# One decode layer on one core: the tail after the last attention head rearranged (order of the last loads, form of the w2 products, output rows, spare products)

## The chip, the cores and the metric

The kernel runs on one core of one Trainium2 chip. The metric is device time in microseconds (us), the median of several executions. A profile's span is some 1.8 us shorter than the device time of the same execution, so spans are compared with spans and times with times. In the views PE is TensorE, which does the matrix products, and PEld its loading of weights; DVE, ACT and POOL are the vector, scalar and GpSimd engines, and SP issues the loads. The granted clock is the share of its full clock (1.00) that TensorE was allowed.

## The reference, cut to what matters

One token is decoded: a modulated layernorm, attention with 8 key/value heads over a cache of 32768 positions, and a feed-forward part with relu.

```python
mod = (silu(c) @ w_mod)                       # six vectors of 512: sa, ca, ga, sb, cb, gb
h = layernorm(x) * (1 + ca) + sa
x = x + ga * (attention(h @ wq, k_cache, v_cache) @ wo)   # wq 512x4096, wo 4096x512
h = layernorm(x) * (1 + cb) + sb
x = x + gb * (relu(h @ w1) @ w2)              # w1 512x1792, w2 1792x512
```

The caches are 134 MB of bf16; with the weights 149.4 MB are read. Everything from "@ wo" on is small work that needs the last head's result. It is called the tail here.

## The kernel before

All loads go through one queue on SP in a fixed order, into a ring of four slots of 4 MB. A load waits until the earlier user of its slot is done.

```python
WOP = [(0, Hkv // 2), (Hkv // 2, Hkv // 4), (3 * Hkv // 4, Hkv // 4)]   # wo in three parts, by heads
W2P = [(0, FA - 3), (FA - 3, 2), (FA - 1, 1)]                          # w2 in three pieces
ring = ctx.enter_context(tc.tile_pool(name="ring", bufs=4))
...
stream += [("v", LAST, (0, 1)), ("v", LAST, (2,)), ("wo", 0), ("v", LAST, (3,)), ("wo", 1), ("wo", 2)]
stream += [("w1",)] + [("w2", i) for i in range(len(W2P))]
```

P·V of a head is done with 512-column products, whose result (`o_ps`) has to be gathered by `blocks` (four operations on DVE) and `o_cols` (a product) into columns. Only the last quarter of the last head is done with 64 small products that write the columns at once. The w2 products go to four column groups: the four of a block write partitions 0, 32, 64 and 96 and run side by side. `normalise` and `spread` then prepare the columns for the products with wo. Part 0 of wo gives rows, which `join_rows` turns into columns; this is done around the wait for the last V.

```python
pv(LAST, (2,))
blocks(LAST)
project(0)            # wo, part 0: 16 row products
o_cols(LAST)
join = join_rows()
next(join)            # copy of the rows on ACT
pv(LAST, (3,))        # 64 small products, straight into the columns
next(join); next(join)
normalise(LAST)
for _ in join: pass
for i in range(1, len(WOP)): project(i)
# ... x1T, layernorm, w1 products into hidT, then w2 on four column groups:
nc.tensor.matmul(ffn_ps[32 * i:32 * i + 1, :], lhsT=hidT[:, ft:ft + 1], rhs=w2_sb[:, a, b, i * P:(i + 1) * P], ...)
# ... two DVE operations, then the output from partitions 0, 32, 64, 96:
nc.scalar.dma_start(out=out[0, 0].rearrange("(i n) -> i n", i=KT), in_=o_bf[:].rearrange("(i r) n -> i r n", r=32)[:, 0, :])
```

## Time and profile before

| | before |
|---|---|
| time, median (3 runs) | 355.85 us (355.77 to 356.11) |
| span of the profiled execution | 354.3 us |
| transfers | 149.4 MB, 432 to 433 GB/s in the middle |
| clock of TensorE over the span | 0.919 |
| x1T starts / w1's products / w2's last product ends | 343.40 / 346.05 to 347.70 / 350.86 us |

The last product group is 24 products, 16 of the next to last piece and 8 of the last; the 8 start at 350.48 only, and the page's list of DMA issues has 7.1 us from issue to landing for that piece, which was issued at 343.40. So the last landing was near 350.4. The transfers themselves still moved a little until about 350.2.

### The profile page before, as it was taken

How to read it: one execution, taken by the hardware profiler on the slowest of the kernel's cores; microseconds unless marked ns; L12 is line 12 of the kernel's file. 1: busy time of each engine (PE TensorE's matmuls, PEld its weight loads, DVE VectorE, ACT ScalarE, POOL GpSimd, SP SyncE). 2: the span in 40 equal slices, each digit the busy share in tenths (PEclk: the TensorE clock that was granted, in tenths of full speed). 3: DMA queues.
4: the chain of work that ended last, by engine and by line, in shares of the span. 5: the costliest groups of instructions: out<-in, count | busy, mean ns of one | idle time of the engine just before them, and what ended most of it. 6: DMA issues, size and time to landing. Idle time of an engine off the chain costs nothing. (4 is left out here: it accounts for less than half of the span.)

```text
span 354.3 us, 4169 instructions
## 1 busy us (share of the span) xinstructions
PE 276.4 (78%) x1403; PEld 114.0 (32%) x1403; DVE 205.8 (58%) x266; ACT 28.9 (8%) x70; POOL 8.4 (2%) x14
## 2 busy tenths in 40 slices
PE   0453793799798979897979796989789787989884
PEld 0121231233233323332333233333333233333373
DVE  8537683973848366571949177553938095843221
ACT  1023004000110011001100101010100010010110
POOL 9000000000000000000000000000000000000000
PEclk9966867699899999999999998899999999999955
DMA  8999999999999999999999999999999999999994
GB/s 313 449 422 455 420 426 451 422 429 425 446 429 414 459 425 416 459 422 422 455 422 425 442 433 426 436 436 422 425 451 425 422 453 425 422 455 403 424 418 164
DMA packets 6613, 149.61 MB, mean 422 GB/s; under 512 B 712, under 2 KB 712, under 8 KB 1608
## 3 DMA queue, kind: packets, MB, share of 16 engines
q1 hardware_dynamic: 6592, 149.43, 98.2%
q8 instruction: 9, 0.15, 0.1%
q14 instruction: 4, 0.03, 0.0%
q10 hardware_dynamic: 8, 0.00, 0.0%
HBM read 149.42 MB, written 0.00 MB: 422 GB/s over the span
## 5 line engine op out<-in xcount | busy, mean ns | idle before, releaser
L398 DVE STREAM_TRANSPOSE KTt<-Ksb 128x2048 f32<-128x2048 f32 x64 | 143.3, 2283 | 61.9 <-DMA Ksb<-in_A_k_cache_dram 52.6
L489 PE MATMUL o_ps<-Vsb,PT_g 128*16 (+1 forms) x496 | 124.9, 387 | 23.4 <-ACT qbd L382 7.8
L418 PE MATMUL S_ps<-KTt,qbd 128*128 128x512 bf16 x512 | 124.1, 395 | 17.9 <-DVE KTt L398 16.2
L418 PEld LDWEIGHTS <-qbd 128*128 128x128 bf16 x512 | 50.0, 100 | 83.3 <-issue 27.4
L489 PEld LDWEIGHTS o_ps<-Vsb,PT_g 128*16 x416 | 36.4, 87 | 90.9 <-issue 66.4
L424 DVE TENSOR_SCALAR_CACHE_REDUCE S_g<-S_ps 128x512 f32<-128x512 f32 x16 | 11.1, 691 | 29.2 <-PE S_ps L418 29.2
L382 ACT COPY qbd<-qrep_sb 32x128 bf16<-32x128 bf16 x32 | 9.4, 295 | 137.1 <-PE S_ps L418 136.0
L461 DVE STREAM_TRANSPOSE PT_g<-P_g 128x1024 bf16<-128x1024 bf16 x8 | 9.7, 1218 | 6.5 <-ACT P_g L455 6.5
L452 ACT ACTIVATE nbias<-Mb_ps 128x1 f32<-128x1 f32 x8 | 1.4, 171 | 130.8 <-PE Mb_ps L450 130.8
L489 PEld LDWEIGHTS <-PT_g 128*16 128x16 bf16 x80 | 6.9, 90 | 10.1 <-issue 0.8
L219 PE MATMUL xc_ps<-cx_sel,cx_bd 16*128 16x2 bf16 x4 | 0.3, 172 | 12.1 <-DVE cx_bd L213 12.1
L455 ACT ACTIVATE P_g<-S_g,nbias 128x1024 bf16<-128x1024 f32 x8 | 9.2, 1149 | 0.2
L520 DVE SCALAR_TENSOR_TENSOR Y<-o_ps,smask,Y 16x128 f32<-16x128 f32 x24 | 8.0, 335 | 0.8
L159 DVE COPY sel<-ident_bf 128x128 bf16<-128x128 bf16 x4 | 7.5, 3688 | 0.0
L541 DVE TENSOR_TENSOR oT_sb<-acc_ps,Linv 128x4 bf16<-128x4 f32 x8 | 1.2, 151 | 9.4 <-PE acc_ps L528 5.6
L467 PE MATMUL L_ps<-Lexp,ones_f 128*128 128x4 f32 x16 | 3.0, 258 | 4.3 <-DVE Lexp L464 4.3
L439 DVE TENSOR_REDUCE Mrow<-mT_ps 1x4 f32<-1x128 f32 x8 | 2.1, 257 | 6.9 <-PE mT_ps L436 6.9
L355 PE MATMUL q_ps<-wq_sb,hT 128*1 128x512 bf16 x32 | 3.6, 625 | 3.0 <-DVE hT L270 3.0
L436 PE MATMUL mT_ps<-ident_f,m_p 128*1 128x128 f32 x8 | 2.2, 270 | 3.9 <-DVE m_p L433 2.0
L467 PEld LDWEIGHTS L_ps<-Lexp,ones_f 128*128 128x128 f32 x16 | 3.1, 222 | 5.7 <-issue 5.1
L287 PE MATMUL mod_ps<-wm_sb,siluT 128*1 128x512 bf16 x24 | 3.4, 612 | 1.2 <-DVE siluT L281 1.2
L510 DVE MEMSET o_ps<- 16x512 f32 x8 | 3.9, 485 | 0.8
(115 smaller groups left out, 84.4 us busy)
## 6 DMA issues: line engine op xcount, KB each, us to landing
Ksb<-in_A_k_cache_dram SPq DMA_DIRECT2D x16, 4096.0 KB, 29.8
Vsb<-in_A_v_cache_dram SPq DMA_DIRECT2D x15, 4096.0 KB, 24.2
wq_sb<-in_A_wq_dram SPq DMA_DIRECT2D x1, 4096.0 KB, 18.7
Vsb<-in_A_v_cache_dram SPq DMA_DIRECT2D x2, 2048.0 KB, 17.9
wm_sb<-in_w_mod_dram SPq DMA_DIRECT2D x1, 3072.0 KB, 10.3
wo_sb<-in_A_wo_dram SPq DMA_DIRECT2D x1, 2048.0 KB
wo_sb<-in_A_wo_dram SPq DMA_DIRECT2D x2, 1024.0 KB, 8.0
w_sb<-in_B_w_dram SPq DMA_DIRECT2D x1, 1792.0 KB, 10.7
```

What stands on the lines that cost most here:

```text
L159: nc.vector.tensor_copy(out=sel[:, hp, :].rearrange("p (a c) -> p a c", a=4), in_=src)
L355: nc.tensor.matmul(q_ps[i][32 * a:32 * a + 1, :].rearrange("o (h e) -> o h e", e=32), lhsT=hT[:, kt:kt + 1], rhs=wq_f[:, kt, i, a], start= ...
L382: nc.scalar.copy(out=o, in_=i)
L398: t = nc.vector.transpose(out=KTt[:].bitcast(F32), in_=Ksb[:, 32 * half:32 * half + 32, :].rearrange("p j d -> p (j d)").bitcast(F32),)
L418: nc.tensor.matmul(S_ps_tiles[g], lhsT=qbd[g % 2][:, hp, s, :], rhs=KTv[:, 16 * sl:16 * sl + 16, h, :, par], start=(t4 == 0 and sl == 0 an ...
L424: nc.vector.tensor_scalar(out=S_tiles[g][:, G, :], in0=S_ps_tiles[g], scalar1=1.0, scalar2=None, op0=ALU.mult, op1=ALU.max, accum_out=m_ti ...
L455: nc.scalar.activation(out=P_g[:], in_=S_g[:].rearrange("p g f -> p (g f)"), func=ACT.Exp, bias=nbias[:], scale=scale, accum_out=l_g[:],)
L461: nc.vector.transpose(out=PT_g[:], in_=P_g[:])
L467: nc.tensor.matmul(L_ps[:], lhsT=ones_f[:], rhs=Lexp[:], start=True, stop=True)
L489: nc.tensor.matmul(o_tiles[g][:], lhsT=PT, rhs=Vx, start=False, stop=False, skip_group_check=True)
L510: nc.vector.memset(o_tiles[g][:], 0.0)
L520: nc.vector.scalar_tensor_tensor(out=Y[:], in0=o[:, s], scalar=smask[:, s:s + 1], in1=Y[:], op0=ALU.mult, op1=ALU.add,)
```

## The change

Its intent: V of the last head complete earlier, only a small part of wo left after it; the last landing of w2 followed by few products; the output read from neighbouring partitions; and products without use ("spare", 22 of them) that keep TensorE at full clock through the waits of the tail. Besides, the whole tail is put in program order, w1 is loaded in two parts and its products are ordered by quarters of the input (kt), and the copy of x1's rows moves from ACT to DVE. The diff, cut to its core:

```diff
-    WOP = [(0, Hkv // 2), (Hkv // 2, Hkv // 4), (3 * Hkv // 4, Hkv // 4)]
+    WOP = [(0, Hkv // 2), (Hkv // 2, Hkv // 4), (Hkv - 2, 1), (Hkv - 1, 1)]
+    WOROWS = 2
-    W2P = [(0, FA - 3), (FA - 3, 2), (FA - 1, 1)]
+    W2P = [(0, 2, slice(0, FB)), (2, FA - 5, slice(0, FB)), (FA - 3, 1, slice(0, FB)), (FA - 2, 1, slice(0, FB)),
+           (FA - 1, 1, slice(0, 1)), (FA - 1, 1, slice(1, FB))]
+    W1P = [(0, KT - 1), (KT - 1, KT)]
@@ the queue (w2's last four pieces get buffers of their own)
-    stream += [("v", LAST, (0, 1)), ("v", LAST, (2,)), ("wo", 0), ("v", LAST, (3,)), ("wo", 1), ("wo", 2)]
+    stream += [("v", LAST, (0, 1)), ("v", LAST, (2, 3))] + [("wo", i) for i in range(len(WOP))]
@@ spare products
+    def keep_clock(n):
+        for _ in range(n):
+            nc.tensor.matmul(spare[0], lhsT=ident_bf[:], rhs=qbd[0][:, 0, 0:4, :], start=True, stop=True)
@@ the tail
-        pv(LAST, (2,))
+        pv(LAST, (2, 3))
         blocks(LAST)
         project(0)
+        keep_clock(2)
         o_cols(LAST)
-        join = join_rows() ... pv(LAST, (3,)) ...
+        keep_clock(4)
         normalise(LAST)
+        project(1)          # now rows, like part 0
+        keep_clock(3)
+        join_rows()         # all of it here
+        keep_clock(1)
+        project(2)
+        keep_clock(2)
+        project(3)
+        ... keep_clock(4); layernorm_T(...); keep_clock(3); w1 by kt with 2 spares; relu; keep_clock(1)
@@ w2: block-diagonal columns of h, one column group, four neighbouring rows
-                        ffn_ps[32 * i:32 * i + 1, :], lhsT=hidT[:, ft:ft + 1],
+                            ffn_ps, lhsT=hid_bd[:, ft, i, :], rhs=w2_sb[:, a, b - bs.start, i * P:(i + 1) * P],
-        in_=o_bf[:].rearrange("(i r) n -> i r n", r=32)[:, 0, :],
+    nc.scalar.dma_start(out=out[0, 0].rearrange("(i n) -> i n", i=KT), in_=o_bf[:])
```

More of the change, by code (lines that the diff above doesn't have):

```diff
@@ L104, in load @@
         elif kind == "w1":
-            t = ring.tile([P, KT, Dff], BF16, tag="slot", name="w1_sb")
-            src = w1_v
-        else:
-            a0, n = W2P[key[1]]
-            t = ring.tile([P, n, FB, D], BF16, tag="slot", name="w2_sb")
-            src = w2_v[:, a0:a0 + n]
+            k0, k1 = W1P[key[1]]
+            t = ring.tile([P, k1 - k0, Dff], BF16, tag="slot", name="w1_sb")
+            src = w1_v[:, k0:k1]
+        else:
+            a0, n, bs = W2P[key[1]]
+            if key[1] < 2:
+                t = ring.tile([P, n, FB, D], BF16, tag="slot", name="w2_sb")
+            else:
+                t = const.tile([P, n, bs.stop - bs.start, D], BF16, name=f"w2_sb{key[1]}")
+            src = w2_v[:, a0:a0 + n, bs]
         stream_dma(t[:], src)
@@ L129 @@
             stream += [(kind, gg, (2 * G, 2 * G + 1)) for kind, gg in (("k", g + 1), ("v", g))]
-    stream += [("v", LAST, (0, 1)), ("v", LAST, (2,)), ("wo", 0), ("v", LAST, (3,)), ("wo", 1), ("wo", 2)]
-    stream += [("w1",)] + [("w2", i) for i in range(len(W2P))]
+    stream += [("v", LAST, (0, 1)), ("v", LAST, (2, 3))] + [("wo", i) for i in range(len(WOP))]
+    stream += [("w1", i) for i in range(len(W1P))] + [("w2", i) for i in range(len(W2P))]
     pos = [0]
@@ L197 @@
     )
-    rowpick = const.tile([P, P], F32)
-    nc.gpsimd.memset(rowpick[:], 0.0)
+    rowpick = const.tile([P, KT], F32)
     nc.vector.tensor_reduce(
-        out=rowpick[:].rearrange("p (j m) -> p j m", m=32)[:, :, 0],
-        in_=ident_f[:].rearrange("p (j m) -> p j m", m=32), op=ALU.add, axis=AX.X,
-    )
+        out=rowpick[:], in_=ident_f[:].rearrange("p (j m) -> p j m", m=32), op=ALU.add, axis=AX.X,
+    )
+    hid_bd = const.tile([P, FT, KT, KT], BF16)
+    nc.gpsimd.memset(hid_bd[:], 0.0)
     rowsum = const.tile([P, 1], F32)
@@ L249, in layernorm_T @@
         stat_ps = small_ps([P, 2], f"stat_ps_{tagp}")
-        m = nc.tensor.matmul(stat_ps[:], lhsT=onesD_f[:], rhs=stat_in[:], start=True, stop=True)
-        tc.stamp_issue_order_token(m.ins, "pe_tail")
+        nc.tensor.matmul(stat_ps[:], lhsT=onesD_f[:], rhs=stat_in[:], start=True, stop=True)
         nu = const.tile([P, KT], F32, name=f"nu_{tagp}")
@@ L261, in layernorm_T @@
         std = const.tile([P, 1], F32, name=f"std_{tagp}")
-        a = nc.scalar.activation(out=std[:], in_=negvar[:], func=ACT.Sqrt, bias=eps_t[:], scale=-1.0)
-        tc.stamp_issue_order_token(a.ins, "act_tail")
+        nc.scalar.activation(out=std[:], in_=negvar[:], func=ACT.Sqrt, bias=eps_t[:], scale=-1.0)
         cen = const.tile([P, KT], F32, name=f"cen_{tagp}")
@@ L313, with four_rows @@
         )
-    def rows32(src_T, name):
+    def four_rows(src_T, name, copy):
         e = const.tile([P, 32, KT], F32, name=f"{name}_exp")
@@ L322, in rows32 @@
         )
-        r_ps = bank(f"{name}_ps")[:, 0:P]
-        m = nc.tensor.matmul(
+        r_ps = bank(f"{name}_ps")[0:KT, 0:P]
+        nc.tensor.matmul(
             r_ps, lhsT=rowpick[:], rhs=e[:].rearrange("p m kt -> p (m kt)"), start=True, stop=True,
         )
-        tc.stamp_issue_order_token(m.ins, "pe_tail")
-        rows = const.tile([P, P], F32, name=f"{name}_rows")
-        a = nc.scalar.copy(out=rows[:], in_=r_ps)
-        tc.stamp_issue_order_token(a.ins, "act_tail")
+        rows = const.tile([KT, P], F32, name=f"{name}_rows")
+        copy(out=rows[:], in_=r_ps)
         return rows
-    gb_rows = rows32(modT_sb[:, 5 * KT:6 * KT], "gb")
+    gb_rows = four_rows(modT_sb[:, 5 * KT:6 * KT], "gb", nc.scalar.copy)
     hT = const.tile([P, KT], BF16)
@@ L477, in pv @@
         Vs = [need(("v", g, u)) for u in us]
-        if g == LAST and us[0] == NTILE - 1:
-            for j in range(TK):
-                c0 = REP * (4 + j // 16)
-                nc.tensor.matmul(
-                    oT_ps, lhsT=Vs[0][:, j, :], rhs=PT_g[:, j % 16, c0:c0 + REP],
-                    start=False, stop=(j == TK - 1), skip_group_check=True,
-                )
-            return
         def step(u, V, PT, Vx):
@@ L523, in blocks @@
         Y_tiles[g] = Y
-        if g == LAST:
-            nc.vector.memset(oT_ps, 0.0)
     def o_cols(g):
         nc.tensor.matmul(
-            oT_ps, lhsT=Y_tiles.pop(g)[:], rhs=qsel, start=(g < LAST), stop=(g < LAST), skip_group_check=True,
+            oT_ps, lhsT=Y_tiles.pop(g)[:], rhs=qsel, start=True, stop=True, skip_group_check=True,
         )
@@ L568, in project @@
         for r in range(n):
-            if i == 0:
+            if i < WOROWS:
                 nc.tensor.matmul(
                     a_rows[0][32 * (r % 4):32 * (r % 4) + 1, :], lhsT=o2_tiles[i][:, r:r + 1],
-                    rhs=wo_sb[:, r, :], start=False, stop=(r >= n - 4), skip_group_check=True,
+                    rhs=wo_sb[:, r, :], start=False, stop=(i == WOROWS - 1 and r >= n - 4), skip_group_check=True,
                 )
@@ L588, in join_rows @@
         for ko in range(KT):
-            yield
             nc.tensor.matmul(
@@ L593, in join_rows @@
             )
+    spare = []
+    def keep_clock(n):
+        if not spare:
+            spare.append(bank("spare_ps"))
+        for _ in range(n):
+            nc.tensor.matmul(spare[0], lhsT=ident_bf[:], rhs=qbd[0][:, 0, 0:4, :], start=True, stop=True)
     with tc.manual_schedule(engines={mybir.EngineType.PE, mybir.EngineType.DVE}):
@@ L661 @@
         normalise(LAST - 1)
-        pv(LAST, (2,))
+        pv(LAST, (2, 3))
         blocks(LAST)
         project(0)
+        keep_clock(2)
         o_cols(LAST)
-        join = join_rows()
-        next(join)
-        pv(LAST, (3,))
-        next(join)
-        next(join)
-        normalise(LAST)
-        for _ in join:
-            pass
-        for i in range(1, len(WOP)):
-            project(i)
-    ffn_ps = bank("ffn_ps")[:, 0:P]
-    nc.vector.memset(ffn_ps, 0.0)
-    stat2 = const.tile([P, 2], F32)
@@ L681 @@
-    x1T = const.tile([P, KT], F32)
-    nc.vector.tensor_tensor(out=x1T[:], in0=attnT_ps, in1=modT_sb[:, 2 * KT:3 * KT], op=ALU.mult)
-    nc.vector.scalar_tensor_tensor(
-        out=x1T[:], in0=x1T[:], scalar=1.0, in1=xT, op0=ALU.mult, op1=ALU.add, accum_out=stat2[:, 0:1],
-    )
-    h2T = const.tile([P, KT], BF16)
-    layernorm_T(x1T[:], stat2, h2T[:], modT_sb[:, 3 * KT:4 * KT], ncb[:], "ln2")
-    x1_rows = rows32(x1T[:], "x1")
-    w1_sb = need(("w1",))
-    w1_f = w1_sb.rearrange("p kt (a m b) -> p kt a b m", m=P, b=FB)
@@ L693 @@
-    hidT_ps = small_ps([P, FT], "hidT_ps")
-    for ft in range(FT):
-        for kt in range(KT):
-            nc.tensor.matmul(
-                hidT_ps[:, ft:ft + 1], lhsT=w1_f[:, kt, ft // FB, ft % FB, :], rhs=h2T[:, kt:kt + 1],
-                start=(kt == 0), stop=(kt == KT - 1),
-            )
-    hidT = const.tile([P, FT], BF16)
-    nc.scalar.activation(out=hidT[:], in_=hidT_ps[:], func=ACT.Relu)
-    for part, (base, n) in enumerate(W2P):
-        w2_sb = need(("w2", part))
-        for a in range(n):
-            for b in range(FB):
-                ft = (base + a) * FB + b
-                for i in range(KT):
+        keep_clock(4)
@@ new lines @@
+        normalise(LAST)
+        project(1)
[5 more added lines that the diff above has]
+        project(3)
+        hidT_ps = small_ps([P, FT], "hidT_ps")
+        nc.vector.memset(hidT_ps[:], 0.0)
+        stat2 = const.tile([P, 2], F32)
+        x1T = const.tile([P, KT], F32)
+        nc.vector.tensor_tensor(out=x1T[:], in0=attnT_ps, in1=modT_sb[:, 2 * KT:3 * KT], op=ALU.mult)
+        nc.vector.scalar_tensor_tensor(
+            out=x1T[:], in0=x1T[:], scalar=1.0, in1=xT, op0=ALU.mult, op1=ALU.add, accum_out=stat2[:, 0:1],
+        )
@@ L708 @@
+        h2T = const.tile([P, KT], BF16)
+        keep_clock(4)
+        layernorm_T(x1T[:], stat2, h2T[:], modT_sb[:, 3 * KT:4 * KT], ncb[:], "ln2")
+        keep_clock(3)
+        for part, (k0, k1) in enumerate(W1P):
+            w1_f = need(("w1", part)).rearrange("p kt (a m b) -> p kt a b m", m=P, b=FB)
+            for kt in range(k0, k1):
+                for ft in range(FT):
                     nc.tensor.matmul(
-                        ffn_ps[32 * i:32 * i + 1, :], lhsT=hidT[:, ft:ft + 1],
@@ L710 @@
-                        rhs=w2_sb[:, a, b, i * P:(i + 1) * P], start=False, stop=(ft == FT - 1),
-                        skip_group_check=True,
-                    )
-    o_rows = const.tile([P, P], F32)
-    nc.vector.tensor_tensor(out=o_rows[:], in0=ffn_ps, in1=gb_rows[:], op=ALU.mult)
-    o_bf = const.tile([P, P], BF16)
-    nc.vector.tensor_tensor(out=o_bf[:], in0=o_rows[:], in1=x1_rows[:], op=ALU.add)
-    nc.scalar.dma_start(
-        out=out[0, 0].rearrange("(i n) -> i n", i=KT),
-        in_=o_bf[:].rearrange("(i r) n -> i r n", r=32)[:, 0, :],
-    )
+                        hidT_ps[:, ft:ft + 1], lhsT=w1_f[:, kt - k0, ft // FB, ft % FB, :], rhs=h2T[:, kt:kt + 1],
@@ new lines @@
+                        start=False, stop=(kt == KT - 1), skip_group_check=True,
+                    )
+                if kt < KT - 2:
+                    keep_clock(1)
+        hb = hid_bd[:]
+        nc.scalar.activation(
+            out=AP(hb.tensor, hb.offset, [hb.ap[0], [KT * KT, FT], [KT + 1, KT]]),
+            in_=hidT_ps[:].unsqueeze(2).to_broadcast([P, FT, KT]), func=ACT.Relu,
+        )
+        x1_rows = four_rows(x1T[:], "x1", nc.vector.tensor_copy)
+        keep_clock(1)
+        ffn_ps = bank("ffn_ps")[0:KT, 0:P]
@@ new lines @@
+        last = len(W2P) - 1
+        for part, (base, n, bs) in enumerate(W2P):
+            w2_sb = need(("w2", part))
+            for a in range(n):
+                for b in range(bs.start, bs.stop):
+                    ft = (base + a) * FB + b
+                    for i in range(KT):
+                        nc.tensor.matmul(
+                            ffn_ps, lhsT=hid_bd[:, ft, i, :], rhs=w2_sb[:, a, b - bs.start, i * P:(i + 1) * P],
+                            start=(part == 0 and a == 0 and b == 0 and i == 0), stop=(ft == FT - 1 and i == KT - 1),
+                        )
@@ L724 @@
+        o_rows = const.tile([KT, P], F32)
+        nc.vector.tensor_tensor(out=o_rows[:], in0=ffn_ps, in1=gb_rows[:], op=ALU.mult)
+        o_bf = const.tile([KT, P], BF16)
+        nc.vector.tensor_tensor(out=o_bf[:], in0=o_rows[:], in1=x1_rows[:], op=ALU.add)
+    nc.scalar.dma_start(out=out[0, 0].rearrange("(i n) -> i n", i=KT), in_=o_bf[:])
 _INS = ['A_x', 'A_k_cache', 'A_v_cache', 'A_wq', 'A_wo', 'B_x', 'B_w1', 'B_w2', 'c', 'w_mod']
```

## The prediction

> **What bounds the kernel now.** I read the page's 40 slices first, then the busy time by stretches, then the chain of waits, and last the timeline of the tail.
>
> ```profile
> PEclk9966867699899999999999998899999999999955
> DMA  8999999999999999999999999999999999999994
> 260.00:300.00 40.00, 33.66 (x144) 12.89 (x143) 23.11 (x26) 1.41 (x3) 0.00 (x0) 1.00 1.00 432
> 336.83:349.85 13.02, 9.86 (x229) 9.20 (x230) 2.24 (x15) 0.96 (x4) 0.00 (x0) 0.53 0.95 389
> ```
>
> The first two lines are the page's slices; the stretches list PE, PEld, DVE, ACT, POOL, the granted clock, the DMA share and GB/s. The transfers are the bound: 149.4 MB pass at 432 to 433 GB/s in every 40 us stretch from 20 to 300 us, and the change moves the same bytes. Only the ends can change. In the last 13 us the rate is 389 GB/s, so 13.02 x (1 - 389/432) = 1.3 us of transfer time is lost there, and TensorE runs at a granted clock of 0.53. After 349.85 us nothing is loaded.
>
> ```profile
> 316.55 5.71 PE o_ps L489 x26
> 322.25 0.03 PE L_ps L467
> 322.29 14.55 DMA Vsb<-in_A_v_cache_dram
> 336.83 0.05 issue
> 336.88 1.81 PE acc_ps L482 x64
> 338.69 0.95 PE acc_ps L590 x4
> ...
> 341.24 1.07 PE acc_ps L576 x32
> 342.31 0.02 issue
> 342.32 7.49 DMA w_sb<-in_B_w_dram
> 349.81 0.04 issue
> 349.85 0.59 PE ffn_ps L708 x16
> ...
> 351.31 0.29 DVE o_bf L716
> ```
>
> The chain (start, length, what) shows that the end is set by the landing of the last piece of w2 at 349.81, which was in the queue behind everything else. From there to the end of the span at 354.3 is 4.5 us: 1.06 products, 0.7 on DVE, and 2.7 from o_bf to the end with the output's DMA. The attention part ends at 343.36, and its second layernorm feeds w1's products just as w1 lands (346.0). So compute and transfers are balanced in the tail: whoever becomes later sets the end.
>
> ```profile
> 323.42 3.83 PE L489 MATMUL o_ps<-Vsb,PT_g 128*16 128x512 bf16 x17 [0.85 <-DVE o_ps L510]
> 335.97 0.38 PE L528 MATMUL acc_ps<-mask_sb,Y 16*128 16x4 f32 x2 [0.76 <-DVE acc_ps L525]
> 343.40 0.16 DVE L682 TENSOR_TENSOR x1T<-acc_ps,modT_sb 128x4 f32<-128x4 f32 x1 [2.86 <-PE acc_ps L576]
> 345.62 0.22 DVE L270 SCALAR_TENSOR_TENSOR h2T<-cen_ln,rstd_ln,modT_sb 128x4 bf16<-128x4 f32 x1
> 346.05 1.65 PE L696 MATMUL hidT_ps<-h2T,w_sb 128*128 128x1 bf16 x56 [0.81 <-DMA w_sb<-in_B_w_dram]
> 348.60 1.02 PE L708 MATMUL ffn_ps<-w_sb,hidT 128*1 128x128 bf16 x32 [0.89 <-DMA w_sb<-in_B_w_dram]
> ```
>
> These timeline lines give my unit costs. A P·V product of 512 columns takes 3.83/17 = 0.22 us at full clock; w1's take 1.65/56 = 0.029 us; w2's in four column groups 1.02/32 = 0.032 us at half clock; x1T to h2T is 345.84 - 343.40 = 2.44 us.
>
> **What the Trainium skill says.** (1) "TensorE: Matmul & The Clock Gate", Part 1: the array runs at half its clock until it has been busy through a window of about 3.4 us, and falls back after idle time. The trace agrees: the granted clock falls to 0.50 at about 337.6, after a stretch with gaps and one-column products. This is what the spare products are for. (2) Same page, "Back-to-back issue gap": N columns take N/2.4 + 2.5 ns at full clock and N/1.2 at half, with a floor of about 25 ns for short ones. The trace agrees for 512 columns (0.216 us between starts, and 0.427 at half clock near 33 us) and nearly for the floor (0.029). (3) "TensorEngine Tiling (Array Packing)", Key Properties: different tiles can work in parallel. The trace agrees: w2's 128-column products start every 0.032 us at half clock, where one alone would stream for 128/1.2 = 107 ns. (4) "DMA: Bandwidth & Descriptors", Where 436 GB/s comes from: a ceiling of 435.2 GB/s; the trace's 432 to 433 is at it, so no order of the transfers makes the middle faster.
>
> **The change part by part.**
>
> *V whole.* The last 2 MB of V no longer stand behind 2 MB of wo, so V is complete 2.10 MB / 0.432 = 4.85 us earlier, at 332.0 instead of 336.83. But TensorE is only through with the first half of that V at 330.4, and now does the second half as 32 products of 512 columns: 32 x 0.218 = 7.0 us, from 332.0 to 338.95. Before, the last 64 small products ended at 338.69. So five microseconds of earlier data buy nothing; P·V ends within 0.3 us of where it did. It loses the small-product form for a quarter of V (1.8 us for what now takes 3.5).
>
> *From P·V to x1T.* blocks() on DVE takes 1.45 (four operations of 0.26 to 0.34): 340.5. Meanwhile project(0), 16 products in about 1.35 us, and 2 spares (0.43): TensorE free at about 340.7. o_cols 0.35: 341.0. Then 4 spares, 0.86: 341.9, where normalise on DVE would have been ready at about 341.6. spread 0.15; project(1), 8 products 0.7: 342.7. 3 spares of 0.65 lie beside the ACT copy of a_sb (0.58 + latency): 343.4. join_rows, 8 f32 passes of 0.15 at full clock (0.26 at half before): 344.6. One spare, 16 products of 0.035, 2 spares, 16 products: 0.22 + 0.56 + 0.43 + 0.56 = 1.8: 346.4. The twelve spares are 2.6 us, of which I count about 1 us on the path (0.25 + 0.22 + 0.43 and a little). So x1T starts at about 346.4, **3.0 us later** than 343.40: the old order had the join and most of its row products out of the way before the last V landed.
>
> *Layernorm.* 2.44 us at half clock, about 2.25 at full (the two stat passes 0.58 to 0.4; the x1_exp operation of 0.28 moved behind h2T). Four spares end as stat's inputs are ready and three lie beside DVE: h2T at 348.65.
>
> *w1.* 56 x 0.029 + 2 spares 0.43 = 2.05: 350.7. relu 0.2, beside it x1's two f32 passes on TensorE (0.3) and one spare: 351.1. The order by kt makes the last quarter of w1 need only 14 products after it lands, but all of it has landed by then.
>
> *w2.* The column groups are given up: all four products of a block write partitions 0 to 3 and stand one behind the other. 56 x 0.056 = 3.1 us at full clock (an estimate: a quarter of the 512-column product, and the page's rule gives the same), 6.0 at half. So 351.1 + 3.1 = 354.2. Before, the whole of w2 was 2 us and half of it was done before the last piece came. The last piece now has 4 products instead of 16, worth 0.8 us, **if** TensorE is waiting for it. By my sums it is not.
>
> *Transfers.* w1 waits for wo's slots (project(0), project(1)), w2 for project(2) and project(3); with these later, gaps of some 1 to 1.5 us open in the queue and the last byte lands at about 351 instead of 349.8: still earlier than TensorE needs it.
>
> *End.* Two DVE operations, 0.45; from o_bf to the end 2.7, perhaps 2.3 with adjacent partitions. 354.2 + 0.05 + 0.45 + 2.5 = 357.2, against 354.3: **+2.9 us**. If short products go at 25 ns at full clock (136 of them save 0.4) and the join takes 1.0, some 0.6 us of that is gone; a few waits that I add up may lie beside each other. I take +2.0 and get 355.85 + 2.0 = 357.9 us.
>
> **Rivals.** (a) *The tail stays bound by the transfers*: if h2T comes at 347 or earlier, TensorE waits for w2, the end follows the last landing by 4 products instead of 16 and the strided output goes: about -1 to -1.5 us, 354.5. For it: the six pieces with 128 KB at the end make sense only then, so its author may have seen it. Against: TensorE's queue above is 7.4 us from P·V to x1T, and w2 alone 3.1. (b) *The spares don't hold the clock*: from 339 to 346 they and the row products stream 4 + 12 + 2 = 18 times 0.213 = 3.8 us of 7. Before, the stretch before the fall at 337.6 had about a third; near 290 to 297 about half was enough. If it falls at the layernorm, w2 costs 6 instead of 3.1, join and stat their old times: +3 us more, 361. (c) *The transfers starve*: if issue to first byte is near 2 us, w2's last bytes come at 352 to 353, after which only a few products follow: about 358, the same time by another cause.
>
> **Range and chances.** The middle of the kernel can't move, since bytes and rate are the same, so all lies within a few us of 355.85. I give 0.6 to my sum (356.5 to 359.5), 0.2 to (a), 0.2 to (b). This gives 357.6 and 354.6 to 361.2. Faster by over 2% would be under 348.7, before the last byte can land: 0.01. Slower by over 2% is over 363: needs half clock through all of the tail and starved transfers: 0.03. Within 2%: 0.96.
>
> **What would show it right or wrong.** Right: P·V of the last head ending near 339; x1T starting at 345.5 to 347; the w2 products 0.054 to 0.06 us apart at clock 1.00 with no wait for the transfers ahead of the last ones; the chain of the end going through TensorE from the last V to the output, not through the last w2 transfer; the middle at 432 GB/s. Wrong: TensorE waiting for w2 in the chain (a); PEclk 5 in the last slices (b); a last landing after 352 (c).

## The result, and the profile after

The changed kernel took 361.69 us (median of 6 runs, 359.92 to 364.14), the kernel before in the same rounds 356.03 (355.77 to 356.16). The ratio is 1.0163, with a 95% interval of 1.0127 to 1.0200. Ratios in this document are the mean time of one kernel's runs over that of the other's of the same rounds, so not quite the ratio of the medians quoted. The change makes the kernel 5.8 us slower (0.0163 x 356), about 0.5 us beyond the end of the stated range, and it makes the time less steady.

The first view is the page's 40 slices of the changed kernel: granted clock in tenths, and GB/s.

```profile
PEclk9995887699999999999999999999789999999988
GB/s 333 424 451 422 445 419 429 440 422 447 420 447 425 440 425 424 444 422 447 422 447 424 440 422 424 445 418 451 422 444 429 433 427 422 451 418 425 329 304 79
```

The middle is unchanged: over 100 to 300 us the rate is 432 to 434 GB/s in each 40 us stretch, as before. The last slices have a higher clock than before (8 in place of 5) but a rate of only 304 to 329 GB/s. The chain of waits of the changed kernel (start, length, what) shows what sets the end:

```profile
331.63 6.63 PE o_ps L483 x30
...
340.63 0.97 PE spare_ps L593 x4
...
342.89 1.96 PE acc_ps L581 x8
...
346.45 0.50 PE acc_ps L568 x16
346.95 0.24 issue
347.19 1.49 PE spare_ps L593 x3
348.68 0.23 PE stat_ps_ln L258 x2
...
350.19 0.49 PE hidT_ps L694 x14
...
352.94 4.62 PE ffn_ps L716 x56
...
357.90 0.28 DVE o_bf L723
```

Before, the last wait in the chain was for a transfer of w2. Now, after the last V at 331.63, no transfer is in it any more: it goes through TensorE and DVE to the output. P·V ends at 338.71, as before (338.69), although V was complete five microseconds earlier. The join of the rows (L581) takes 1.96 us on the path. Three spare products stand between x1T and the layernorm's sums (L258). And w2's products take 4.62 us without a wait.

The stretches of the changed kernel (columns: length; busy time of PE, PEld, DVE, ACT, POOL; granted clock; DMA share; GB/s) show the clock and the transfers of the tail:

```profile
338.00:340.00 2.00, 1.84 (x21) 0.55 (x16) 1.16 (x4) 0.00 (x0) 0.00 (x0) 1.00 0.51 182
...
342.00:344.00 2.00, 2.00 (x12) 1.39 (x9) 0.00 (x0) 1.79 (x2) 0.00 (x0) 1.00 0.88 275
344.00:346.00 2.00, 2.00 (x23) 1.60 (x24) 0.00 (x0) 0.07 (x1) 0.00 (x0) 0.88 0.80 312
346.00:348.00 2.00, 1.76 (x20) 0.97 (x19) 0.58 (x6) 0.00 (x0) 0.00 (x0) 0.50 0.78 306
...
354.00:356.00 2.00, 2.00 (x24) 2.00 (x22) 0.00 (x0) 0.00 (x0) 0.00 (x0) 0.56 0.00 0
```

From 342 to 346 PE was busy for 4.00 of 4.00 us, spares among it, and still the clock fell to half at about 345.5. It came back near 348.9, fell again near 352.3, just ahead of w2's products, and came back near 355.7. These four changes lie 3.4 us apart each. The transfers sag to 182 GB/s around 339 and stay near 310: the last part of wo, w1 and w2 wait, themselves or behind one another in the queue, for slots that TensorE now frees late. They end at about 353, more than 4 us before TensorE is through, so this costs nothing yet.

The output's DMA, by the timeline of each kernel:

```profile
351.64 1.10 ACTq L717 DMA_DIRECT2D out_dram<-o_bf  x1
```

```profile
358.21 0.55 ACTq L724 DMA_DIRECT2D out_dram<-o_bf  x1
```

Before (the first), the issue took 1.10 us and the span ended 2.70 us after the last DVE operation (351.60 to 354.3); after (the second) 0.55 and 2.2 us (358.18 to 360.4). This part of the change does gain what was hoped for, 0.5 us.

### The profile page after: what moved, and what is told of

Its sections match the earlier page's. It is cut to its first block, busy times and chain, and to the rows that moved or that the text cites. A ratio compares the mean times of both kernels' runs of the same rounds, so it can differ in the third digit from the quotient of the medians.

```text
span 360.4 us, 4078 instructions
## 1 busy us (share of the span) xinstructions
PE 283.4 (79%) x1351; PEld 117.0 (32%) x1354; DVE 206.9 (57%) x270; ACT 28.8 (8%) x69; POOL 8.5 (2%) x14
## 5 line engine op out<-in xcount | busy, mean ns | idle before, releaser
L483 PE MATMUL o_ps<-Vsb,PT_g 128*16 (+1 forms) x512 | 128.0, 382 | 24.2 <-ACT qbd L385 7.6
L483 PEld LDWEIGHTS <-PT_g 128*16 128x16 bf16 x96 | 8.4, 90 | 12.5 <-issue 1.2
L593 PE MATMUL spare_ps<-qbd,ident_bf 128*128 128x512 bf16 x19 | 6.7, 447 | 0.4 <-issue 0.4
L512 DVE TENSOR_SCALAR Y<-o_ps,smask 16x128 f32<-16x128 f32 x8 | 2.2, 270 | 7.3 <-PE o_ps L483 7.3
L716 PE MATMUL ffn_ps<-w_sb,hid_bd 128*4 128x128 bf16 x56 | 4.6, 262 | 0.5 <-ACT hid_bd L701 0.5
```

The costliest lines, as they stand in the source:

```text
L483: nc.tensor.matmul(o_tiles[g][:], lhsT=PT, rhs=Vx, start=False, stop=False, skip_group_check=True)
L593: nc.tensor.matmul(spare[0], lhsT=ident_bf[:], rhs=qbd[0][:, 0, 0:4, :], start=True, stop=True)
L716: nc.tensor.matmul(ffn_ps, lhsT=hid_bd[:, ft, i, :], rhs=w2_sb[:, a, b - bs.start, i * P:(i + 1) * P], start=(part == 0 and a == 0 and b = ...
```

## The experiments

Theory 1: a queue of work on TensorE from the last P·V to the output sets the end; V whole, the serial w2 products and the late join made it longer, and the spares don't pay. Rival A: the spares alone are the loss. Rival B: the late issues of w1 and w2 set the end. All runs gave correct results, with 4 to 6 executions each. The ratio is to the kernel before in the same rounds.

| run | what | median us | ratio (95% interval) |
|---|---|---|---|
| changed kernel | | 361.69 | 1.0163 (1.0127 to 1.0200) |
| e1_no_spares | no spares | 361.20 | 1.0149 (1.0133 to 1.0164) |
| e2_w2_groups | w2 in column groups | 360.44 | 1.0122 (1.0105 to 1.0140) |
| e3_v_parts | V in parts | 359.68 | 1.0116 (1.0099 to 1.0133) |
| e4_one_slot | everything issued early | 360.78 | 1.0133 (1.0117 to 1.0148) |
| g4_early_join_alone | no spares, early join | 360.94 | 1.0133 (1.0112 to 1.0153) |
| f3_v_parts_w2_groups | e3 and e2 | 359.48 | 1.0093 (1.0080 to 1.0106) |
| g2_parts_groups_no_spares | f3 without spares | 358.31 | 1.0065 (1.0041 to 1.0088) |
| g3_and_early_join | g2 with early join | 357.86 | 1.0053 (1.0030 to 1.0075) |
| h1_g3_one_slot | g3, everything issued early | 356.25 | 1.0006 (0.9992 to 1.0019) |
| f1_before_bd | before, block-diagonal w2 | 358.04 | 1.0056 (1.0043 to 1.0069) |
| f2_before_spares | before, spares in its waits | 356.84 | 1.0016 (1.0004 to 1.0028) |
| f4_before_best | f2, small last piece, output from SP | 356.03 | 1.0007 (0.9991 to 1.0024) |
| g1_before_last_piece | before, small last piece | 355.90 | 0.9996 (0.9982 to 1.0010) |
| h2_before_one_slot | g1, everything issued early | 355.87 | 1.0000 (0.9987 to 1.0014) |

**The spares taken out (e1).**

```diff
     def keep_clock(n):
-        if not spare: ...
-        for _ in range(n):
-            nc.tensor.matmul(spare[0], ...)
+        return
```

> The changed kernel with its spare products taken out, nothing else. Theory 1 (a queue of products on TensorE from the last P.V to the output sets the end; the spares buy clock at about the price they cost): x1T starts about 1 us earlier, near 346.0 instead of 346.99, the layernorm loses its 0.9 us wait behind spares, but the clock stays at half from about 342 on and w2's 56 products take 6.0 instead of 4.6 us: 359.5 to 362 us, within 2 us of the changed kernel's 361.7. Rival A (the spares are the loss): 357 to 358.5. Rival B (the transfers, held back by late issues at 310 GB/s, set the end): no change, 361 to 362, with w1 or w2 waiting for a landing.

Measured 361.20 us, as theory 1 expects; rival A falls. By the chain of this run x1T starts at 346.04 instead of 346.99 and h2T is there at 348.50 instead of 350.14. But the clock falls near 345.5 in both profiled executions (0.88 over the same stretch, below and in the table of stretches above), so the spares ahead of it did not delay the fall; nor did it come at 342, as expected. What the spares bought in these two traces is the stretch at full clock from 348.9 to 352.3. Without them the clock stays at half from 345.5 to about 355.7, and the products of w2 (second line, timeline) take a microsecond longer:

```profile
344.00:346.00 2.00, 2.00 (x37) 1.91 (x36) 0.00 (x0) 0.16 (x1) 0.00 (x0) 0.88 0.95 385
```

```profile
350.62 5.71 PE L713 MATMUL ffn_ps<-w_sb,hid_bd 128*4 128x128 bf16 x56
```

So with V whole and a serial w2, the 22 spares cost about what they buy. They also spread the times: 360.89 to 361.44 without them, 359.92 to 364.14 with them. The changed kernel's fastest execution had a granted clock of 0.956 over the span, its slowest 0.929, which suggests that it changes from run to run how much of the tail is at full clock. That is not shown: one execution's trace was kept, and the clock over the span contains the start of the kernel too.

**w2 in four column groups (e2).**

```diff
-    ffn_ps, lhsT=hid_bd[:, ft, i, :], rhs=w2_sb[...]
+    ffn_ps[32 * i:32 * i + 1, :], lhsT=hidT[:, ft:ft + 1], rhs=w2_sb[...]
-    in_=o_bf[:]
+    in_=o_bf[:].rearrange("(i r) n -> i r n", r=32)[:, 0, :]
```

> The changed kernel with w2 in four column groups and the strided output rows as before, six pieces and all else kept. Theory 1: w2's 4.6 us shrink to 1.0 to 2.0, but the last pieces land only at 353.3, so the products end near 354.5; the output's end takes 0.5 us more: 359 to 360 us, 2 to 2.5 less than the changed kernel. Rival B: the end follows the last landing in both, no more than 0.5 us less.

Measured 360.44 us, 1.5 us less than the changed kernel by the ratios (0.0041 x 356), where 2 to 2.5 were expected; the intervals of the two runs still overlap a little, so the traces and f1 have to carry the reading. In the trace w2's 56 products take 1.67 us instead of 4.62, and the output's end 2.84 instead of 2.2. That is 2.3 us of gain in the tail; P·V began 0.9 us later in this execution (332.53, by its chain), which is outside the part that was changed. The column groups also need a memset of `ffn_ps`. In the program order of this tail it stands behind the copy of x1's rows and ends at 353.46 only; w2's first product starts at 353.55. In the kernel before it is done before the tail.

**V in parts again (e3).**

```diff
-    stream += [("v", LAST, (0, 1)), ("v", LAST, (2, 3))] + ...
+    stream += [("v", LAST, (0, 1)), ("v", LAST, (2,)), ("wo", 0), ("v", LAST, (3,))] + ...
-        pv(LAST, (2, 3))
+        pv(LAST, (2,))
         blocks(LAST); project(0); keep_clock(2); o_cols(LAST); keep_clock(4)
+        pv(LAST, (3,))          # 64 small products, as before
         normalise(LAST)
```

> The changed kernel with the last head's V in three parts again (half, quarter, wo's first part, quarter; the last quarter by 64 small products straight into the columns), wo still in four parts, spares kept. Theory 1: P.V ends at the same 338.7 but what follows it at once is normalise, since blocks (1.45) and o_cols (0.4) lie before the last landing: x1T about 1.9 us earlier, 359.3 to 360.5 us. If V whole were the gain that it was meant to be, this would be slower than 361.7. If the end is set by the transfers: no change.

Measured 359.68 us, 1.7 us less by the ratios; expected 1.2 to 2.4. The intervals just overlap, but the trace agrees: V whole is a loss. Data that arrives five microseconds earlier meets a TensorE that is still busy, and loses the form that needs no gathering. In the trace normalise starts at 339.43 instead of 340.67, and x1T at 345.77 instead of 346.99; this is what the order gains, 1.2 us. This run's w2 products fell into a stretch at clock 1.00 and show what they cost there, 0.059 us each (this saves another 1.3 us in the profiled execution, which isn't owed to V):

```profile
351.50 3.29 PE L728 MATMUL ffn_ps<-w_sb,hid_bd 128*4 128x128 bf16 x56 [0.25 <-ACT hid_bd L713]
```

**Everything issued early (e4).** The last two parts of wo, w1 and two pieces of w2 lie side by side in one ring slot.

```diff
-    t = ring.tile([P, k1 - k0, Dff], BF16, tag="slot", name="w1_sb")
+    t = in_tail([k1 - k0, Dff])       # a view into one slot of 32 KB per partition
```

> The changed kernel with the last two parts of wo, w1 and the first two pieces of w2 side by side in one ring slot, so that they are all issued from 330.5 us on instead of one by one until 349.7; PE's order is unchanged. Theory 1: the transfers run at over 400 GB/s to the end and the last one lands near 350 instead of 353.3, and the time does not move: 361 to 362.5 us. Rival B (late issues set the end): 358 to 359.

Measured 360.78 us, just under the 361 to 362.5 of theory 1. The transfers did what was intended, in the stretch where the changed kernel had 182 GB/s:

```profile
338.00:340.00 2.00, 1.84 (x21) 0.64 (x20) 1.02 (x3) 0.00 (x0) 0.00 (x0) 1.00 1.05 433
```

They were over by 350 us, 10 us before the end, and the profiled execution took 362.3 us, just as long as the changed kernel's; it was the slowest of its four. The median is 0.9 us lower, but the intervals overlap. Rival B falls as the bound of the changed kernel. (It comes back below, once TensorE's queue is shorter.)

**The block-diagonal w2 alone, on the kernel before (f1).**

```diff
-    ffn_ps[32 * i:32 * i + 1, :], lhsT=hidT[:, ft:ft + 1], ...
+    ffn_ps, lhsT=hid_bd[:, ft, i, :], ...       # w2 in its three old pieces, all else as before
```

> The kernel before with one part of the change alone: w2 by block-diagonal columns of h on one column group, four adjacent output rows; w2 in its three old pieces, V, wo and the rest as before, no spares. Theory 1 (serial products): hid is ready near 348, the 56 products at half clock take 5.7 us as in the run without spares, so they end at 354 instead of 350.9; the output's end is 0.5 shorter: 358 to 359 us, +2.5. If the part were the gain that it was meant to be: under 355.5.

Measured 358.04 us, +2.0 us. The timeline of this run:

```profile
348.31 5.21 PE L710 MATMUL ffn_ps<-w_sb,hid_bd 128*4 128x128 bf16 x56 [0.89 <-DMA w_sb<-in_B_w_dram]
```

They wait once, for w2's first piece, and then run serially until 353.5, long past the last landing. Of the 2.7 us which that costs against 350.9, the neighbouring output rows give back 0.4: from the last DVE operation to the end of the span it is 2.3 us here.

**Spares in the waits of the kernel before (f2).**

```diff
         project(0)
+        keep_clock(3)
         o_cols(LAST)
+        keep_clock(2)
+        ... keep_clock(2) before and keep_clock(6) after the layernorm's sums, keep_clock(2) beside relu
```

> The kernel before with 15 spare products put only where its TensorE waits anyway (3 during blocks, 2 before the last V lands, 2 and 6 around the layernorm's sums, 2 beside relu), tail in program order. Theory 1: the clock stays near 1.00 for longer, attention and layernorm end some 0.5 to 1 us earlier, but the end waits for the last piece of w2 near 350.4 all the same: 355.2 to 356.2 us, at most 0.5 faster. If half clock were what the kernel before suffers from: 354 or less.

Measured 356.84 us, 0.6 us slower: a miss. The run also puts the tail in program order, so the 0.6 us are not surely the spares' alone, and its profiled execution was its slowest (358.03; the others 355.95 to 356.88). In it the spares did not hold the clock. The first line is a stretch of this run, the second its timeline:

```profile
340.00:342.00 2.00, 1.48 (x8) 1.40 (x9) 0.72 (x4) 0.00 (x0) 0.00 (x0) 0.54 1.03 431
```

```profile
345.50 2.72 PE L602 MATMUL spare_ps<-qbd,ident_bf 128*128 128x512 bf16 x6
```

The clock fell near 340.2, during the join's products; the 64 small products just ahead of them ran at full clock. From then on a spare takes 0.43 us instead of 0.22, so that six of them, meant to fill 1.3 us, stood in w1's way for 2.7.

**V in parts and column groups together (f3).** The edits of e3 and e2 on the changed kernel.

> The changed kernel with both undone: the last head's V in three parts and w2 in column groups; wo in four parts, the late join and the spares stay. Theory 1: the two add up to about 3.2 us (1.7 and 1.5 alone), 358 to 359 us, unless the last landing of w2, which the late issues put near 353, now sets the end and eats a part. The rest to 356.0 is then the late join and the spares ahead of the layernorm.

Measured 359.48 us, the ratio at 3.3 us above before (0.0093 x 356). The two gave 1.7 and 1.5 us alone and give 2.5 together, less than their sum, and the time lies 0.5 us above the 358 to 359 expected. Two causes are left, the spares and the order of the tail.

**Without spares (g2), and with the early join (g3).**

```diff
 # g2: f3 with keep_clock emptied.  g3: besides
-    WOROWS = 2
+    WOROWS = 1
-        o_cols(LAST); pv(LAST, (3,)); normalise(LAST); project(1); join_rows(); project(2); project(3)
+        o_cols(LAST); join = join_rows(); next(join); pv(LAST, (3,)); next(join); next(join)
+        normalise(LAST); the rest of join; project(1); project(2); project(3)
```

> The changed kernel with V in three parts, w2 in column groups and no spares: of the change only wo in four parts, the late join with two row parts, the six pieces and w1 by kt remain. Theory 1: about 1 to 2 us less than with spares (359.48): 357 to 358.5; what is left above before is the late join (copy 0.6, join 2.0, row products 0.6 on the path behind normalise). If the spares were worth their price here, it would be no faster than 359.5.

> As the one without spares, and the join early again, with wo's second part in column products as before. Of the change only the four parts of wo, two parts of w1 by kt and six pieces of w2 remain. Theory 1: back at the kernel before, 355.6 to 356.4 us, 1.5 to 2 less than the one with the late join. If something else of the change costs time, it stays above 357.

g2 took 358.31 us: here, where w2 doesn't depend on the clock so much, the spares are a loss of about 1.0 us (0.0093 to 0.0065; the intervals overlap a little, so it is only just clear of the noise). g3 took 357.86; it was to be 355.6 to 356.4, a second miss. By the traces the early join works: x1T starts at 343.25 in g3, 344.70 in g2, 343.40 in the kernel before. But the gain does not reach the end (the intervals of g2 and g3 overlap), because w2's products wait three times for transfers. Two of the lines of g3's timeline:

```profile
349.36 0.59 PE L724 MATMUL ffn_ps<-w_sb,hidT 128*1 128x128 bf16 x16 [1.35 <-DMA w_sb<-in_B_w_dram]
...
351.88 0.99 PE L724 MATMUL ffn_ps<-w_sb,hidT 128*1 128x128 bf16 x16 [0.25 <-DMA w_sb<-in_B_w_dram]
```

The last landings of w2 come at 351.9 and after, in place of 350.4.

**The early join alone (g4).** The same edit of the tail on the changed kernel without spares, with V whole and the block-diagonal w2.

> The changed kernel without spares (361.2) with the early join and wo's second part in column products; V whole and block-diagonal w2 stay. Theory 1: in the run without spares P.V's end to x1T took 7.0 us, of which copy, join and row products 3.2; early, about 2 of these lie beside blocks and normalise: 359 to 360 us. Rival (the join hides behind w1's late landing anyway): 361.

Measured 360.94 us against 361.20 without the early join: no difference that the intervals would allow, nearer to the rival. In its timeline w1's products wait for w1:

```profile
348.33 1.66 PE L692 MATMUL hidT_ps<-h2T,w_sb 128*128 128x1 bf16 x56 [1.67 <-DMA w_sb<-in_B_w_dram]
```

x1T is 0.6 us earlier (345.45), and the late landing of w1 takes most of that back.

**Issued early, with TensorE's queue short again (h1).** g3 with the one slot of e4; number and size of the pieces stay.

> As the run with V in parts, column groups, no spares and the early join (357.86), and besides wo's last two parts, w1 and the first two pieces of w2 side by side in one ring slot, issued from 334 us on; the number and size of the pieces are the same. Theory 1 with late issues as the last remainder: the last w2 landing comes back from 352.6 to 350 and the time to 355.5 to 356.2 us. If the pieces' number or wo in four parts costs it: no less than 357.5.

Measured 356.25 us, ratio 1.0006: the last 1.7 us are gone (0.0053 to 0.0006). The rate is 394 GB/s or more in every 2 us stretch from 338 to 348, and w2's 56 products run through without a wait for a transfer; what they wait for now is the late memset of `ffn_ps` on DVE:

```profile
349.06 1.02 PE L743 MATMUL ffn_ps<-tail_sb,hidT 128*1 128x128 bf16 x32 [0.57 <-DVE ffn_ps L735]
```

So the late issues were the remainder, not the number of pieces, nor wo in four parts, nor the tail in program order, which this run keeps.

**Attempts to beat both (g1, f4, h2).** The kernel before with the last 256 KB of w2 in two pieces (g1); with the spares and the output from SP besides (f4); with everything issued early (h2).

```diff
-    W2P = [(0, FA - 3), (FA - 3, 2), (FA - 1, 1)]
+    W2P = [(0, FA - 3, slice(0, FB)), (FA - 3, 2, slice(0, FB)), (FA - 1, 1, slice(0, 1)), (FA - 1, 1, slice(1, FB))]
-    nc.scalar.dma_start(            # f4 only
+    nc.sync.dma_start(
```

> The kernel before with the last 256 KB of w2 as two pieces of 128 KB in buffers of their own, nothing else: the part of the six pieces that still looks useful, without spares. Theory 1: after the last landing 4 products instead of 8, and the next to last piece is not held by a slot: 355.3 to 355.9 us, 0 to 0.2% faster, the only way to beat both kernels that these runs point to. Slower only if smaller pieces land later.

> The run with spares in the waits of the kernel before, plus the last piece of w2 cut in two of 128 KB in buffers of their own, and the output's DMA issued from SP instead of ACT; column groups kept. Theory 1: after the last landing 4 products instead of 8 at full clock (-0.3), the output's issue 0.33 instead of 1.10 (-0.5): 354.8 to 355.6 us, 0.1 to 0.3% faster than before. Rival: the output's DMA costs its landing, not its issue, and nothing is gained.

> The kernel before with the last 256 KB of w2 in two pieces, and wo's last part, w1 and w2's first piece in one ring slot, the rest of w2 in buffers of their own, so that everything is issued by 337 us. Theory 1: the small dips of the transfers at 334 and 342 to 346 us are gone, the last landing 0.2 to 0.6 us earlier: 355.3 to 355.8 us. Rival: the queue was never empty before, and nothing changes, 355.9.

All three are equal to the kernel before within their intervals; the gains that I had hoped for did not come. f4 shows one thing more: issued from SP the output's DMA occupies its queue for 0.62 us instead of 1.10, but the span still ends 2.68 us after the last DVE operation, as before. So the rival was right: the output's cost with strided rows is not its issue. And it corrects f2: with the same spares the clock fell near 340.3, but came back near 347, and w2's products ended at 350.39 instead of 350.86. This was the fastest of its six executions (355.56 to 357.38); so these spares brought the clock back in one trace and not in the other, and the median gains nothing.

## Why the prediction was wrong

Its direction was right, and so was the outline of the mechanism: the middle did not move, P·V ended where it had (338.71, forecast 338.95), the end went from the transfers to TensorE's queue. It gave 357.6 us and a range up to 361.2; measured were 361.69. Term by term, from the changed kernel's profile:

| term | forecast | measured | difference |
|---|---|---|---|
| x1T starts | 346.4 | 346.99 | +0.6 |
| x1T to h2T | 2.25 | 3.14 | +0.9 |
| w1's products with two spares | 2.05 | 1.98 | -0.1 |
| relu to w2's first product | 0.4 | 0.77 | +0.4 |
| w2's products | 3.1 | 4.62 | +1.5 |
| from w2's end to the end of the span | 3.0 | 2.8 | -0.2 |

**The step that failed** is "56 x 0.056 = 3.1 us at full clock", with the layernorm "about 2.25 at full" and the spares that "end as stat's inputs are ready": all three take for granted that the spares hold the clock. They did not. w2 ran for more than half of its time at half clock, and of the four spares ahead of the layernorm's sums most took 0.43 us, so that the sums started at 348.47, although their inputs were complete by 347.56. The 0.4 between relu and w2 fits this too: the weights of the last spare were loaded at 352.40, at half clock, and w2 started at 352.94 (the spare itself is missing from the trace, so this is not shown). e1 and e3 show the two ends: 5.7 us for w2 almost all at half clock, 3.3 at full. This was rival (b), at 361 us the nearest of all numbers in the forecast; I gave it 0.2. The reasoning for it counted the streaming time of the spares (3.8 of 7 us) and took "about half" for enough. f2 repeats that error on the kernel before. The trace of the kernel before should have warned: the prediction reads the fall at 337.6 as one after idle time, but PE was busy for 2.11 of the 3.40 us ahead of it, and its longest gap was 0.76 us.

**Smaller errors.** The join's f32 passes were put at "0.15 at full clock (0.26 at half before)". By the timelines they take 2.03/8 = 0.25 us at full clock too, and 1.07/4 = 0.27 at half: I had carried over the cost of another f32 product. The loads of their weights fill this time (1.94 us for the eight). The weights are read with a step of four elements; whether that is the reason was not tested. The join is 0.8 us over its forecast, and two spares at half clock behind it (0.86 instead of 0.43) add 0.4; the join began 0.5 earlier than forecast. Together this is most of x1T's 0.6. And the sum was +2.9 us, but "I take +2.0" took a discount for waits that might overlap; the measurement gives +5.8, and there was no evidence for a discount. Two slips have no weight: the changed tail has 88 short products (32 of wo, 56 of w1), not 136, and the mean of the three cases with their chances is 357.8, not 357.6.

**The rivals.** (a), that the transfers keep the bound, did not happen. (c), that the transfers starve, is half right: the rate fell to near 310 GB/s, but e4 shows that this does not set the changed kernel's end. It is hidden behind TensorE's queue and comes out only after that has been shortened (g3, h1).

**Where the 5.8 us are**, by undoing one after the other, from the ratios: V whole and the serial w2 together 2.5; spares 1.0; late join 0.4, inside the error of the measurement; late issues 1.7; 0.2 is left, also inside the error. The late memset of the column groups (0.57 us without a product in g2 and h1) is contained in these values. They are the values in this order. In another order they differ, since each is hidden behind the one that is taken away before it: the spares cost 0.5 when taken out first, and the late issues 1.1 at most. What stays open is what exactly the clock counts, and so whether some other number of spares would have held it. One hint, not tested: in the 3.4 us before the fall at 345.5 PE was busy throughout, but spares took only 1.2 us of it and mostly one-column products the rest; in the 3.4 us at whose end the clock came back (348.9) spares took 2.6.

## What to carry to other kernels

Before an arrival is moved forward, look at whether the consumer is free then: TensorE was busy with the half before, and the earlier V only cost the cheap form for the last quarter. Give up column groups only where the products are not on the path: 56 products of 128 columns went from 1.7 us on four groups to 3.3 to 5.7 on one. Spare products for the clock are to be proved by the granted clock in the trace, not by counting; where they fail each costs twice its time (0.43 instead of 0.22 us), and a load that waits for a ring slot is delayed by whatever is put into the queue ahead of the slot's release.

## What the Trainium skill lacked or had wrong

- "TensorE: Matmul & The Clock Gate", the table on why this matters for kernels, asks for no idle gaps over some 3 us to stay at full clock. In the changed kernel PE was busy 4.00 of 4.00 us from 342 to 346 and the granted clock fell to 0.50 at about 345.5. The page does not say how one-column products, f32 passes and column groups count towards the activity.
- "DMA: Bandwidth & Descriptors", Rules for kernel authors, wants transfers of 1 MiB and more for the full rate. Issued early enough, pieces of 256 to 512 KB in the queue with one of 1344 KB ran at 400 to 433 GB/s (e4, 338 to 348 us); issued late, the same pieces ran at 275 to 331 (changed kernel, 340 to 352 us).
- I found no page with the cost of an output of four rows by the step of its partitions: 1.10 us of issue and 2.70 to the end from partitions 0, 32, 64, 96; 0.55 and 2.2 from four neighbouring ones. Issued from SP, the strided form took 0.62 us of issue and the same 2.68 to the end.
